# Forty-eight partitions of wq loaded in transfers of eight partitions: a decode kernel of attention and MLP on one core

## The chip, the cores and the metric

The kernel runs on one core of a Trainium2 chip. The metric is the device time of one execution in microseconds (us); lower is better. A profile is one more execution, recorded by the hardware profiler. Its times count from the span's start, which is the first instruction.

## What is computed

One decode step: attention with a cache (A) and a small MLP (B), mixed by a gate, for 8 batch rows of 448 values in bf16. A uses the last 1,024 positions of the caches; 16 query heads share 8 heads of K and V.

```python
# x: 8 x 1 x 448; k_cache, v_cache: 8 x 8 x 4096 x 256; wq: 448 x 4096; wo: 4096 x 448
def _A_ref(x, k_cache, v_cache, wq, wo):
    W = min(4096, max(256, Sk // 4))                      # 1024
    q = (x @ wq).reshape(B, Sq, Hq, Dh).transpose(0, 2, 1, 3)
    k = jnp.repeat(k_cache[:, :, Sk - W:, :], rep, axis=1)
    v = jnp.repeat(v_cache[:, :, Sk - W:, :], rep, axis=1)
    p = softmax(jnp.einsum("bhqd,bhkd->bhqk", q, k) * Dh ** -0.5)
    o = jnp.einsum("bhqk,bhkd->bhqd", p, v)
    return o.transpose(0, 2, 1, 3).reshape(B, Sq, Hq * Dh) @ wo
def _B_ref(x, w1, b1, w2, b2):
    return gelu(layernorm(x) @ w1 + b1) @ w2 + b2
g = sigmoid((x * gate_w).sum(-1, keepdims=True))
out = g * a + (1 - g) * b
```

## The kernel before

Nearly all large loads are issued from SyncE's queue, in program order: w1, its remainder w1_t and w2 (L159 to L164), then wq (L165 to L168), then K, V and wo in the order of the list `units` (L170 to L200). wq has 448 rows of 4,096 columns. Its first 384 rows lie in the tile `wq_sb`, of 128 partitions: partition p holds rows 3p, 3p + 1 and 3p + 2, which are one run of 24,576 bytes in memory. L167 loads it in three transfers (DC is 3), the c-th of which takes row 3p + c, 8,192 bytes, into every partition. The other 64 rows are `wq_t` (L168), half a row in each partition.

K and V come in 64 units of 1 MB, two batch rows of one head at a time, as 128 partitions of 8,192 bytes (`load`, L141). The last unit of V comes as two halves. A pool of 12 buffers takes them; `issue_to` (L182) issues a load when a buffer has been read. The eight parts of wo, 448 KB each, are issued between them (L187); wo's last part is the last load of all. The framework gives the loads eight semaphores in turn, so a load waits until the load that had the same semaphore before it has landed. The three small loads at the start (x, b1 and b2, L156 to L158), the load of gate_w (L288, eight copies of a row into eight partitions) and half of the output go through ScalarE's queue, and take semaphores from the same eight.

TensorE works in the order of the program: the MLP (L311, L347), then q (L370 to L384), where the rounds c = 0, 1 and 2 read `wq_sb[:, c, :]` on all partitions and the fourth reads `wq_t`, then the steps over K and V. One step of K transposes half a unit (L407), VectorE copies it (L412), and 16 small matmuls give scores (L433). After the four units of a head comes the softmax (L444 to L496), and with a lag of three steps the products with V (L508), the scaling (L519) and the projection with wo (L533), which adds into one bank. At the end VectorE mixes A and B (L577) and two transfers write the output (L581).

Of the kernel before, what the change touches and what calls it, by code (L numbers as in the profile page):

```python
# [16 lines left out]
def kernel(  # L17
# [15 lines left out]
    nc = tc.nc  # L33
    P = nc.NUM_PARTITIONS
# [73 lines left out]
    wq_sb = big.tile([P, DC, HD], BF16, name="wq_sb")  # L108
# [54 lines left out]
    w2_v = w2_sb[:].rearrange("p (h k) n -> p h k n", h=2)  # L163
    nc.sync.dma_start(w2_v, B_w2.rearrange("(h p k) n -> p h k n", h=2, k=NH))  # L164
    wq_v = A_wq[0:DM, :].rearrange("(p c) n -> p c n", c=DC)  # L165
    for c in range(DC):
        nc.sync.dma_start(wq_sb[:, c, :], wq_v[:, c, :])  # L167
    nc.sync.dma_start(wq_t[:], A_wq[DM:D, :].rearrange("r (h n) -> (r h) n", h=2))  # L168

    VU = (SPG + LAG) // TB  # L170
# [441 lines left out]
```

## Time and profile before

| | |
|---|---|
| time, median of 3 runs | 196.78 us (196.78 to 196.85) |
| the profiled execution's own time | 196.92 us |
| its span | 195.2 us |
| granted TensorE clock, mean | 0.768 |
| TensorE busy | 164.2 us (84%) |
| VectorE busy | 113.1 us (58%) |
| bytes moved by DMA | 78.14 MB, 400 GB/s on average |
| wq_sb loads: count, size, median us to landing | 3, 1,024 KB, 12.1 |
| K loads: count, size, median us to landing | 32, 1,024 KB, 18.3 |

In the rows of the profile, PE is TensorE, PEld its weight loads, DVE VectorE, ACT ScalarE, and SPq and ACTq are the queues of SyncE and ScalarE from which DMAs are issued. The page gives each engine's busy share, the DMA queues with their packets, megabytes and the share of 16 engines' span that the packets took, and the chain of work that ended last. A row of a table by stretches has the stretch and its length, each engine's busy time with the number of instructions, the granted clock, the mean busy share of the 16 DMA engines and GB/s. Behind a row of the timeline stands, in brackets, the idle time before it and what ended that.

### The profile page before, as it was taken

To read this page: it belongs to the slowest core of one execution; us is meant where nothing else is said; L and a number is where in the kernel's file an instruction comes from. 1 tells how busy PE (TensorE), PEld (TensorE's weight loads), DVE (VectorE), ACT (ScalarE), POOL (GpSimd) and SP (SyncE) were. 2 spreads that over 40 slices of the span, in tenths; PEclk is the share of its full clock that TensorE was granted. 3 is DMA by queue.
4 is the path that set the end of the run, shared out by engine and by line. 5 is a ranking of instruction groups with operands and counts; after the bars stand their busy time and mean duration, and the time that the engine had idled before them with its cause. 6 is when DMAs were issued, how large, how long until landed. Compare 5 with 4: busy or idle time off the path is not lost.

```text
span 195.2 us, 7355 instructions
## 1 busy us (share of the span) xinstructions
PE 164.2 (84%) x3417; PEld 153.6 (79%) x3417; DVE 113.1 (58%) x255; ACT 6.4 (3%) x13; POOL 2.8 (1%) x16
## 2 busy tenths in 40 slices
PE   2677799988899796958999898988898989989752
PEld 1565799988899796957999797978897989989541
DVE  3122189996477653764559674964586646766401
ACT  5000000000000000010000000000000000000000
POOL 5000000000000000000000000000000000000000
PEclk9999889997569855585569996995599655699555
DMA  6999999999999999999999999999999999999940
GB/s 215 412 426 425 425 413 426 426 423 420 421 426 422 417 425 426 425 417 431 423 423 419 422 425 428 418 421 418 425 430 417 421 425 430 426 420 425 394 176 5
DMA packets 12769, 78.14 MB, mean 400 GB/s; under 512 B 1330, under 2 KB 3523, under 8 KB 4164
## 3 DMA queue, kind: packets, MB, share of 16 engines
q1 hardware_dynamic: 12688, 77.67, 95.4%
q8 instruction: 26, 0.43, 0.8%
q10 hardware_dynamic: 52, 0.02, 0.0%
q14 instruction: 3, 0.02, 0.0%
HBM read 77.68 MB, written 0.01 MB: 398 GB/s over the span
## 4 chain that ended last, share of the span: by engine, by line
DMA 91%; PE 6%; SPq 1%; issue 0%; DVE 0%
DMA kv<-in_A_k_cache_dram 47%; DMA kv<-in_A_v_cache_dram 19%; DMA wo_sb<-in_A_wo_dram 18%; DMA wq_sb<-in_A_wq_dram 7%; PE ktp L407 4%; PE grp L433 1%; PE A_bank L533 0%; PE grp L508 0%; SPq L167 0%; PE grp L422 0%; SPq L164 0%; DVE res L577 0%; SPq L159 0%; SPq L162 0%; SPq L148 0%
## 5 line engine op out<-in xcount | busy, mean ns | idle before, releaser
L412 DVE COPY kt<-ktp 128x1024 bf16<-128x1024 bf16 x128 | 84.4, 687 | 44.4 <-PE ktp L407 43.9
L407 PE MATMUL ktp<-ident,kv 128*128 128x128 bf16 x1024 | 89.0, 257 | 7.9 <-DMA kv<-in_A_k_cache_dram 6.7
L407 PEld LDWEIGHTS <-kv 128*128 128x128 bf16 x1024 | 78.0, 118 | 10.9 <-DMA kv<-in_A_k_cache_dram 7.9
L508 PE MATMUL grp<-e,kv 128*128 128x4 bf16 x1024 | 35.6, 166 | 2.6 <-DMA kv<-in_A_v_cache_dram 2.5
L508 PEld LDWEIGHTS <-kv 128*128 128x128 bf16 x1024 | 32.6, 101 | 5.6 <-DMA kv<-in_A_v_cache_dram 2.8
L433 PE MATMUL grp<-qT,kt 128*128 128x4 bf16 x1024 | 36.6, 166 | 0.3 <-DVE kt L412 0.2
L433 PEld LDWEIGHTS <-kt 128*128 128x128 bf16 x1024 | 34.6, 100 | 1.8 <-issue 0.6
L482 ACT ACTIVATE e<-grp 128x256 bf16<-128x256 f32 x8 | 3.1, 383 | 161.8 <-PE grp L475 161.8
L491 PE MATMUL A_bank<-zs,onesf 128*128 128x16 f32 x16 | 3.6, 299 | 4.5 <-DVE zs L487 4.5
L491 PEld LDWEIGHTS A_bank<-zs,onesf 128*128 128x128 f32 x16 | 2.8, 218 | 5.1 <-DVE zs L487 5.1
L533 PE MATMUL A_bank<-wo_sb,ot 128*8 128x224 bf16 x64 | 5.5, 305 | 0.8 <-DMA wo_sb<-in_A_wo_dram 0.5
L321 PE MATMUL h_ps<-yT,w_sb 128*128 128x8 bf16 x42 | 4.2, 195 | 1.2 <-DMA w_sb<-in_B_w_dram 1.2
L495 DVE RECIPROCAL rz<-A_bank 128x16 f32<-128x16 f32 x8 | 2.1, 258 | 5.4 <-PE A_bank L491 5.4
L519 DVE TENSOR_TENSOR ot<-grp,rz 128x32 bf16<-128x32 f32 x8 | 1.5, 186 | 6.4 <-PE grp L508 6.4
L487 DVE TENSOR_REDUCE zs<-e 128x16 f32<-128x256 bf16 x8 | 4.8, 602 | 0.0
L353 PE MATMUL b_ps<-w_sb,hT 128*8 128x224 bf16 x28 | 2.8, 388 | 2.4 <-DVE b_ps L349 2.4
L338 DVE COPY z<-h_ps 128x112 f32<-128x112 f32 x1 | 0.3, 275 | 7.7 <-PE h_ps L329 7.7
L321 PEld LDWEIGHTS <-w_sb 128*128 128x128 bf16 x42 | 3.6, 152 | 1.3 <-DMA w_sb<-in_B_w_dram 1.3
L475 PE MATMUL grp<-diag,onesb 128*128 128x256 bf16 x8 | 2.5, 308 | 2.2 <-DVE diag L469 1.9
L353 PEld LDWEIGHTS <-hT 128*8 128x8 bf16 x28 | 1.8, 121 | 3.0 <-DVE hT L344 2.2
L446 DVE TENSOR_REDUCE pm<-grp 128x16 f32<-128x256 f32 x8 | 3.3, 415 | 0.6 <-PE grp L433 0.6
L533 PEld LDWEIGHTS <-ot 128*8 128x8 bf16 x64 | 2.6, 93 | 1.3 <-issue 0.4
(82 smaller groups left out, 53.6 us busy)
## 6 DMA issues: line engine op xcount, KB each, us to landing
kv<-in_A_k_cache_dram SPq DMA_DIRECT2D x32, 1024.0 KB, 18.3
kv<-in_A_v_cache_dram SPq DMA_DIRECT2D x31, 1024.0 KB, 18.3
wo_sb<-in_A_wo_dram SPq DMA_DIRECT2D x8, 448.0 KB, 18.3
wq_sb<-in_A_wq_dram SPq DMA_DIRECT2D x3, 1024.0 KB, 12.1
w_sb<-in_B_w_dram SPq DMA_DIRECT2D x1, 1568.0 KB
w_sb<-in_B_w_dram SPq DMA_DIRECT2D x1, 1344.0 KB, 5.9
kv<-in_A_v_cache_dram SPq DMA_DIRECT2D x2, 512.0 KB, 19.8
wq_t<-in_A_wq_dram SPq DMA_DIRECT2D x1, 512.0 KB, 14.5
```

The costliest lines, as they stand in the source:

```text
L321: nc.tensor.matmul(o, lhsT=cols(w1_sb[:, c, h * FH : (h + 1) * FH]), rhs=yT[:, c, :], start=(c == 0), stop=False,)
L353: nc.tensor.matmul(b_ps[CP * j : CP * j + NB, 0:DN], lhsT=M["hT"][:, k * NB : (k + 1) * NB] if k < NF else onesb[0:1, 0:NB], rhs=w2_sb[:, ...
L407: nc.tensor.transpose(ktp[:, c * P : (c + 1) * P], K[:, h * HC + c, j * P : (j + 1) * P], ident[:],)
L412: nc.vector.tensor_copy(kt[:, j, :], ktp[:])
L433: nc.tensor.matmul(G[g][:, s : s + RU], lhsT=kt[:, j, c * P : (c + 1) * P], rhs=qT[:, j, g, bu * TB : (bu + 1) * TB, :].rearrange("p t i - ...
L446: nc.vector.reduce_max(pm[:], G[g][:, S0 : S0 + NC * R].rearrange("p (c r) -> p r c", r=R), axis=AXIS.X,)
L475: nc.tensor.matmul(G[g][:, S0 : S0 + NC * R].rearrange("p (c r) -> p c r", c=NC), lhsT=onesb[:], rhs=diag[g % 2][:].unsqueeze(1).to_broadc ...
L482: nc.scalar.activation(e[:], G[g][:, S0 : S0 + NC * R], ACT.Exp)
L487: nc.vector.reduce_sum(zs[:], E[g][:].rearrange("p (c r) -> p r c", r=R), axis=AXIS.X)
L491: nc.tensor.matmul(zc, lhsT=onesf[:], rhs=zs[:], start=False, stop=True, skip_group_check=True)
L508: nc.tensor.matmul(G[g][:, o : o + RU], lhsT=V[:, cc, :].rearrange("p (q j) -> p j q", j=NJ)[:, j, :], rhs=E[g][:, cc * R + bu * RU : cc * ...
L533: nc.tensor.matmul(A_bank[CP * j : CP * j + NB, 0:DN], lhsT=ot[:].rearrange("p j (b i) -> p j i b", i=rep)[:, h, i, :], rhs=wo_sb[g][:, k, ...
```

## The change

wq's 128 partitions are divided into partitions 0 to 79 and 80 to 127. The first 80 are still loaded in three transfers, one for each c, now of 80 partitions x 8,192 bytes. The last 48 are loaded in six transfers of eight partitions, each partition its whole run of 24,576 bytes, all three c at once. Two of these stand ahead of each transfer of 80. So nine transfers take the place of three; the bytes are the same. No other line differs, and the lines behind move by ten.

```diff
     wq_v = A_wq[0:DM, :].rearrange("(p c) n -> p c n", c=DC)
+
+
+    SH = 48
+    PM = P - SH
+    small = [(p, p + 8) for p in range(PM, P, 8)]
     for c in range(DC):
-        nc.sync.dma_start(wq_sb[:, c, :], wq_v[:, c, :])
+        for lo, hi in small[2 * c : 2 * c + 2]:
+            nc.sync.dma_start(
+                wq_sb[lo:hi].rearrange("p c n -> p (c n)"),
+                wq_v[lo:hi].rearrange("p c n -> p (c n)"),
+            )
+        nc.sync.dma_start(wq_sb[0:PM, c, :], wq_v[0:PM, c, :])
     nc.sync.dma_start(wq_t[:], A_wq[DM:D, :].rearrange("r (h n) -> (r h) n", h=2))
```

## The prediction

> **What bounds the kernel now.** I read the chain of work that ended last first, then the queues' part of the page, then stretches near the end, then the trace's records of single DMA packets. The chain and the queues, from the page:
>
> ```profile
> DMA 91%; PE 6%; SPq 1%; issue 0%; DVE 0%
> ...
> q1 hardware_dynamic: 12688, 77.67, 95.4%
> q8 instruction: 26, 0.43, 0.8%
> ```
>
> The span ends with a DMA in 91% of its chain, and queue q1, SyncE's, keeps the 16 DMA engines busy for 95.4% of the span. TensorE is busy for 84%, but the chain names it for 6%. So the time is set by the DMA engine that finishes last. Stretches of the tail (first column the stretch in us, last two the mean busy share of the 16 engines and GB/s):
>
> ```profile
> 150.00:180.00 30.00, 27.46 (x585) 26.19 (x582) 18.87 (x38) 0.38 (x1) 0.00 (x0) 0.71 1.02 425
> 180.00:184.60 4.60, 3.04 (x63) 2.36 (x63) 2.26 (x11) 0.38 (x1) 0.00 (x0) 0.50 1.00 412
> 185.50:189.20 3.70, 2.09 (x72) 1.92 (x70) 0.26 (x1) 0.00 (x0) 0.00 (x0) 0.50 0.52 203
> 189.70:190.90 1.20, 0.58 (x16) 0.50 (x16) 0.04 (x1) 0.00 (x0) 0.00 (x0) 0.50 0.09 33
> ```
>
> The engines do not end together: all 16 are busy to 184.6, about eight (0.52 of 16) from 185.5 to 189.2, one or two (0.09) after 189.7. What follows the last of them, from the timeline of the tail:
>
> ```profile
> 191.37 0.91 PE L533 MATMUL A_bank<-wo_sb,ot 128*8 128x224 bf16 x8 [0.54 <-DMA wo_sb<-in_A_wo_dram]
> ...
> 192.32 0.44 DVE L577 SCALAR_TENSOR_TENSOR res<-A_bank,gg,bvec 64x224 bf16<-64x224 f32 x1 [1.26 <-PE A_bank L533]
> 192.79 0.38 SPq L581 DMA_DIRECT2D out_dram<-res  x1
> ```
>
> The last packet of wo ends at 190.98 and lands at 191.33; 3.9 us of fixed tail follow, to 195.2. The profiled execution took 196.92 us, 1.7 more than its span. The median of the runs, 196.78, is 0.07% below it, so I forecast against 196.92 without a correction.
>
> **Which engine ends last, and why.** A packet record has a start, a duration, a queue and a size, but no engine. In the steady part an 8,192 B packet takes 309 ns and the next starts 3 ns before it ends, so packets can be linked into 16 chains by their times. The finish of a transfer on one engine is a 4 B packet. From one 4 B packet to the next, eight 8,192 B packets, is 2.453 us on an undisturbed chain. Two things mark chains:
>
> - The load of gate_w, eight rows on ScalarE's queue, leaves one 896 B packet (41 ns) on each of eight chains between 63.27 and 63.57; there the interval is 2.497. I call these the gate eight.
> - Each of the 26 instruction packets of q8 (16,384 B, about 930 ns) holds up one chain: an interval of 3.87 instead of 2.453, 1.41 us lost. They go round eight chains in turn; two of these take four, the others three.
>
> The ends of the sixteen chains:
>
> ```
> gate eight, no instruction packets   184.68 184.76 184.80 185.14 185.15 186.49
> gate eight, three, and four          189.44 190.23
> the rest, none                       185.13 185.40
> the rest, three (five chains)        189.34 189.39 189.43 189.43 189.60
> the rest, four                       190.98
> ```
>
> These give 8 to 9 busy chains at 187 and 1.4 on average from 189.7 to 190.9, as the stretches do (0.52 and 0.09 of 16). The lateness is the instruction packets: about 4.2 us for three. Two of the eight late chains are among the gate eight. The chain of 190.23 is alone in its phase by over 100 ns, so I am sure of it; that of 189.44 has a neighbour 5 ns away.
>
> **The change, part by part.** *Bytes.* Before, each chain carries 8 rows of 8,192 B of each of three wq transfers: 24 packets. After, the three transfers of 80 rows give each chain 5 rows each, 15 packets; six transfers of eight rows of 24,576 B go to eight chains only, one row each. I take these eight to be the gate eight, since that load too has eight rows. They get 6 x 24,576 B, the bytes of 18 packets, so 33 against 24: nine more, 9 x 306 ns = +2.75 us. The other eight lose nine: -2.75 us. Longer runs may save a little: a 4,096 B packet every 157 ns and an 8,192 B one every 306 make the fixed part some 7 ns, at most 12 x 7 = 0.08 us for six rows.
>
> [...]
>
> *Issues.* SyncE issues nine wq transfers for three: six more at 0.49 us (the median of L167). Eight semaphores are used in turn, so a transfer waits for the one eight before. K's first load now waits for the first 80-row transfer, which the gate eight pass at about 10.6 + 2 x 0.92 + 5 x 0.306 = 14.0 (10.6 is the end of w2). With 0.35 to landing and 1.05 from issue to packets (L159: 0.80 to 1.85), K's packets are there at 15.4. The other eight run dry at 10.6 + 15 x 0.306 + 8 x 0.157 = 16.4. One us of cover; without it those engines would lose time of which they have 2.75 us spare. Cost 0. Later, the other eight run up to 10 us ahead of the last chain; issue to landing is 18.3 us (median of the K loads), so their queues stay filled.
>
> *TensorE.* The q matmuls read all partitions, so the first of three rounds, which began at 18.7, waits for the sixth small transfer at about 19.5. K's transposes stand behind them in TensorE's order; K's first load, on which they waited for 1.33 us until 23.54, lands about 2.7 us later too. TensorE and the copies after it move later with the data. Cost 0 at the end, since the tail waits on wo; if TensorE had no slack to catch up the price would again be at most these 2.7 us, not a sum of both.
>
> *Sum.* Gate eight: 187.4 to 189.2, and the two with instruction packets 192.2 and 190.23 + 2.75 = 192.98. The rest: 182.4 to 186.9 and 188.2. The last end moves from 190.98 to 192.9, +1.9 us. **196.92 + 1.9 = 198.8 us**, 1% slower. The change evens the halves on average, but adds work to the two late chains that stand in the wrong half. Bounds of this case: if the packet count goes round differently, the last is a chain of three, 192.2, giving 198.0; 199.1 with a little more delay at the start.
>
> **The rivals.**
>
> *A. Eight adjacent partitions are a narrow door; slower by far.* Eight engines now write at once into eight neighbouring partitions, which before held for no large transfer. No row shows it at size. The nearest are the 896 B packets: six of x's, into eight neighbouring partitions, began within 18 ns; five took 39 or 40 ns, like lone ones, and the first 61. That speaks for no limit, but so few bytes may only have been buffered. If four rows have to share what one chain moves alone, a row takes 4 x 0.918 = 3.67 us, 2.75 more; six transfers add 16.5 us to the gate eight: 192.9 + 16.5 = 209.4, a time of 215.3 us. Any partial sharing falls between 198.8 and that. [...]
>
> *B. The late chains are all in the other half; faster.* If the eight small-transfer chains hold none of the instruction packets (because SyncE's eight rows go elsewhere than ScalarE's, or these packets use other engines in another execution), the loaded chains end at 186.49 + 2.75 = 189.2 and the late ones at 188.2: 1.8 us earlier, 195.1 us. The tipping point is one late chain of four packets among the eight: it alone makes it slower. For it speaks that six of the eight late chains do stand in the other half; against it the chain of 190.23, marked by both signs.
>
> *C. The small transfers are spread over 16 engines after all.* Then no chain's bytes change and the time stays within 0.2 us of 196.9. Against it: the gate load used eight chains.
>
> **How the numbers follow.** The forecast gets 0.46 (198.0 to 199.1), A in full or part 0.32 (199.5 to 216), B 0.14, C 0.08 and the like. A change of 0.2% is about what a measurement of this kernel can tell from none; the cases give faster 0.14, same 0.07, slower 0.79. To hold 8 in 10 the range takes the forecast, most of A and part of C, leaving out B: 196.7 to 216.
>
> **What would show it.** Right: in the tail, a stretch with two chains (0.12) left after 190, the last wo landing near 193.2, wq's later loads landing some 2.7 us later, and chains of the gate eight with 33 packets' worth of wq. A: packets of the small transfers that take well over 0.92 us per 24,576 B, first K landing 15 us later. B: the last wo landing before 190 and a staircase with a higher second step. Wrong would be the forecast, too, if q8's packets fell on other chains, or if TensorE rather than a DMA released the last o_proj.

## The result, and the profile after

The changed kernel takes 218.07 us (median; 218.04 to 219.41) against 196.81 us of the kernel before, measured beside it: a ratio of 1.110, 95% interval 1.105 to 1.114. It is 21.3 us slower. The forecast was 198.8 us, with a range up to 216.0; the time lies 2.1 us outside, and 2.8 us beyond the price of rival A.

The profiled execution took 218.07 us, its span 216.4. The shares of the chain that ended last, from the page of the kernel after, stand against DMA 91% before:

```profile
DMA 76%; PE 15%; DVE 4%; issue 2%; SPq 1%; ACT 0%
```

The chain in order of time (start, length, what) has two pieces of a new size, both of wq, and its last load is wo, as before:

```profile
3.00 11.78 DMA wq_sb<-in_A_wq_dram
14.80 26.49 DMA wq_sb<-in_A_wq_dram
...
196.47 15.86 DMA wo_sb<-in_A_wo_dram
```

The timeline shows that wo still releases the last projection:

```profile
212.37 0.91 PE L543 MATMUL A_bank<-wo_sb,ot 128*8 128x224 bf16 x8 [0.53 <-DMA wo_sb<-in_A_wo_dram]
```

So a DMA still sets the end: the last wo packet ends at 211.99 instead of 190.98, 21.0 us later, and wq holds the chain until 41.3. In the 40 slices of the span (4.9 us each before, 5.4 us after), the engines' busy tenths and GB/s, before first:

```profile
DMA  6999999999999999999999999999999999999940
GB/s 215 412 426 425 425 413 426 426 423 420 421 426 422 417 425 426 425 417 431 423 423 419 422 425 428 418 421 418 425 430 417 421 425 430 426 420 425 394 176 5
```

and after:

```profile
DMA  6989998999999999999999999999999999999930
GB/s 227 425 108 179 89 197 91 333 423 423 421 420 420 426 421 427 420 424 423 426 421 420 427 420 427 421 423 418 429 423 423 421 423 423 430 420 426 377 149 10
```

The busy row is nearly as full as before; in the row of GB/s five slices, the third to the seventh, fall to 89 to 197. The stretch in which its packets move, and a later one, first in the kernel after (last two columns: busy share of the 16 DMA engines, GB/s):

```profile
10.20:37.50 27.30, 5.95 (x63) 4.59 (x62) 2.17 (x8) 0.30 (x1) 0.00 (x0) 0.71 1.03 141
18.90:25.90 7.00, 0.00 (x0) 0.00 (x0) 0.08 (x1) 0.00 (x0) 0.00 (x0) 0.70 1.03 109
37.50:42.00 4.50, 2.52 (x89) 2.46 (x90) 0.00 (x0) 0.00 (x0) 0.00 (x0) 0.50 0.95 291
60.00:100.00 40.00, 36.24 (x783) 34.35 (x781) 27.46 (x58) 0.77 (x2) 0.00 (x0) 0.79 1.01 422
```

and in the kernel before:

```profile
10.20:37.50 27.30, 23.50 (x482) 21.60 (x481) 14.64 (x30) 0.30 (x1) 0.00 (x0) 0.94 1.01 423
60.00:100.00 40.00, 34.21 (x648) 32.39 (x645) 23.42 (x49) 0.93 (x3) 0.00 (x0) 0.63 1.01 423
```

The share is 1.03 and 1.01, so the engines did not lack work; but what they move fell from 423 GB/s to 141, and from 60 us on it is as before. Nearly all the loss lies in the stretch of wq. From 10.2 to 37.5 the missing bytes are 27.3 us x (423 - 141) GB/s = 7.7 MB, which take 18 us at 423 GB/s; from 37.5 to 42.0 another 1.4 us are lost in the same way. By the packet records the bytes are 19.8 us behind the kernel before from there to the end. The last packet is 21.0 us behind, because the chains of packets are not late by the same amount; the part on the prediction comes back to that. TensorE waits for wq, as its line for q shows, before and after:

```profile
L377 PE MATMUL q_ps<-xT,wq_sb 128*128 128x8 bf16 x96 | 2.6, 167 | 0.0
L387 PE MATMUL q_ps<-xT,wq_sb 128*128 128x8 bf16 x96 | 2.9, 168 | 20.9 <-DMA wq_sb<-in_A_wq_dram 20.9
```

The packet records tell how. The 48 rows of 24,576 B, which three 8,192 B packets' time would make 0.92 us, take 2.01 to 4.10 us, 3.23 on average. Nor are the other packets spared: of the 8,192 B packets between 10 and 45 us, 309 ns each before but for five held up by instruction packets and a few up to 316, 367 of 574 now take over 340 ns. Some 39 lie within 5% of four times 306 ns and 32 within 5% of five times; the others lie below and between, and none takes over 1,572. Packets that take up to five times the normal time, while all engines are busy, look like something shared by up to five.

### The profile page after: what moved, and what is told of

Its sections match the earlier page's. It is cut to its first block, busy times and chain, and to the rows that moved or that the text cites. A ratio compares the mean times of both kernels' runs of the same rounds, so it can differ in the third digit from the quotient of the medians.

```text
span 216.4 us, 7364 instructions
## 1 busy us (share of the span) xinstructions
PE 163.7 (76%) x3417; PEld 152.7 (71%) x3417; DVE 113.1 (52%) x255; ACT 6.4 (3%) x13; POOL 2.8 (1%) x16
## 4 chain that ended last, share of the span: by engine, by line
DMA 76%; PE 15%; DVE 4%; issue 2%; SPq 1%; ACT 0%
DMA kv<-in_A_k_cache_dram 33%; DMA wq_sb<-in_A_wq_dram 18%; DMA wo_sb<-in_A_wo_dram 16%; PE ktp L417 9%; DMA kv<-in_A_v_cache_dram 8%; PE grp L443 2%; DVE kt L422 2%; PE q_ps L387 1%; PE grp L518 1%; PE A_bank L543 1%; SPq L164 1%; DVE gsum L302 0%; PE A_bank L501 0%; DVE diag L479 0%; DVE prod L301 0%
## 5 line engine op out<-in xcount | busy, mean ns | idle before, releaser
L417 PE MATMUL ktp<-ident,kv 128*128 128x128 bf16 x1024 | 87.7, 254 | 7.7 <-DMA kv<-in_A_k_cache_dram 7.4
L417 PEld LDWEIGHTS <-kv 128*128 128x128 bf16 x1024 | 76.8, 117 | 11.1 <-DMA kv<-in_A_k_cache_dram 8.8
L518 PEld LDWEIGHTS <-kv 128*128 128x128 bf16 x1024 | 32.7, 101 | 5.1 <-issue 3.0
L387 PE MATMUL q_ps<-xT,wq_sb 128*128 128x8 bf16 x96 | 2.9, 168 | 20.9 <-DMA wq_sb<-in_A_wq_dram 20.9
L387 PEld LDWEIGHTS <-wq_sb 128*128 128x128 bf16 x96 | 2.7, 104 | 21.2 <-issue 20.8
L399 DVE TENSOR_SCALAR qT<-q_ps 128x128 bf16<-128x128 f32 x2 | 0.5, 298 | 27.3 <-PE q_ps L387 27.3
L543 PE MATMUL A_bank<-wo_sb,ot 128*8 128x224 bf16 x64 | 6.2, 335 | 0.8 <-DMA wo_sb<-in_A_wo_dram 0.5
```

The costliest lines, as they stand in the source:

```text
L387: nc.tensor.matmul(q_ps[:, k * NB : (k + 1) * NB], lhsT=w, rhs=xs, start=(c == 0 and k == 0), stop=(c == DC), skip_group_check=True,)
L417: nc.tensor.transpose(ktp[:, c * P : (c + 1) * P], K[:, h * HC + c, j * P : (j + 1) * P], ident[:],)
L518: nc.tensor.matmul(G[g][:, o : o + RU], lhsT=V[:, cc, :].rearrange("p (q j) -> p j q", j=NJ)[:, j, :], rhs=E[g][:, cc * R + bu * RU : cc * ...
L543: nc.tensor.matmul(A_bank[CP * j : CP * j + NB, 0:DN], lhsT=ot[:].rearrange("p j (b i) -> p j i b", i=rep)[:, h, i, :], rhs=wo_sb[g][:, k, ...
```

## The experiments

The theory, **doors**, was my assumption when the runs were planned; neither kernel's trace shows it by itself. It supposes that groups of four partitions are written through a common door, which passes no more than what one chain moves alone (8,192 B per 306 ns), that a transfer of all 128 partitions is dealt out so that each chain has its own door, and that eight neighbours have two doors, so that four chains wait at each. Rivals: a **long run** of 24,576 B is slow in itself; **reading** neighbouring rows is slow; the **imbalance** of the chains, or the eight semaphores, starves something. The times of the kernel before on the same chips were 196.72 to 196.94 us (medians).

Kernels that change a line of the changed kernel, in the table as "after":

| kernel | us | ratio (95%) | rows of 24,576 B: mean, range, us | longest 8,192 B packet before 60 us, ns |
|---|---|---|---|---|
| after | 218.07 | 1.110 (1.105 to 1.114) | 3.23, 2.01 to 4.10 | 1,572 |
| e1, rows in three packets | 220.74 | measured once | - | 1,611 |
| e2, six apart | 208.32 | 1.060 (1.057 to 1.063) | 1.73, 1.18 to 2.79 | 1,064 |
| e3, 80 and 48 | 204.96 | 1.040 (1.038 to 1.043) | - | 1,078 |
| e4, 16 neighbours | 207.59 | measured once | 2.66, 1.51 to 3.30 | 1,202 |
| e5, written six apart | 208.93 | 1.061 (1.052 to 1.070) | 1.71, 1.08 to 2.66 | 940 |
| e6, written to neighbours | 219.56 | 1.115 (1.112 to 1.118) | 3.22, 2.03 to 3.93 | 1,662 |
| e7, 32 in neighbours | 213.72 | 1.085 (1.072 to 1.099) | 3.17, 2.15 to 3.99 | 1,508 |
| e8, 32, four apart | 204.88 | 1.040 (1.030 to 1.051) | 1.62, 1.11 to 1.86 | 856 |

In every kernel some 8,192 B packets of 760 to 860 ns stand beside an instruction packet, as before.

**e1, the long run taken away.**

```diff
-    wq_sb = big.tile([P, DC, HD], BF16, name="wq_sb")
+    wq_sb = big.tile([P, DC, HD + 32], BF16, name="wq_sb")
...
-                wq_sb[lo:hi].rearrange("p c n -> p (c n)"),
-                wq_v[lo:hi].rearrange("p c n -> p (c n)"),
+                wq_sb[lo:hi, :, 0:HD], wq_v[lo:hi],
...
-        nc.sync.dma_start(wq_sb[0:PM, c, :], wq_v[0:PM, c, :])
+        nc.sync.dma_start(wq_sb[0:PM, c, 0:HD], wq_v[0:PM, c, :])
```

> The six small transfers keep their partitions and bytes, but each row goes as three packets of 8,192 B (wq_sb's rows are padded by 64 B). Doors theory (groups of partitions are written through a common door that moves only what one DMA chain moves, 8,192 B per 306 ns, so four of eight neighbours share one): no change, 216 to 220 us, and these packets take about 4 to 5 x 309 ns = 1.2 to 1.5 us. Rival, long runs (a packet of 24,576 B is slow in itself): packets of 309 ns, about 199 us.

220.74 us, 0.7 above what I expected, packets up to 1.6 us, and 141 GB/s from 10.2 to 37.5, as in the changed kernel. Without any long run nothing is won, so the run's length is not the cause.

**e2, other partitions for the same rows.**

```diff
-    small = [(p, p + 8) for p in range(PM, P, 8)]
+    small = [slice(PM + j, P, 6) for j in range(6)]
...
```

(The loop below takes a slice in place of two bounds.)

> Each small transfer takes eight partitions six apart (80, 86, ... 122) instead of eight neighbours; rows, sizes, counts and order as in the changed kernel. Doors theory: the eight rows reach seven or eight doors, so a row takes 0.92 to 1.84 us instead of 3.2, and the time is 199 to 204 us (198.8 by the bytes per chain, the rest by sharing doors with the other eight chains' own packets). Long runs: 218 us, rows still about 3.2 us. Imbalance alone (half the engines, eight semaphores): 218 us too.

208.32 us: 9.8 us of the 21.3 are gone with nothing changed but which partitions go together, and rows take 1.73 us. Imbalance alone can't do that. Its stretch of wq:

```profile
10.00:27.50 17.50, 6.27 (x66) 4.77 (x65) 2.17 (x8) 0.30 (x1) 0.00 (x0) 1.00 1.03 237
```

The time is 4 us above what I expected of the doors; e3 tells why.

**e3, no eight-row transfer at all.**

```diff
-        for lo, hi in small[2 * c : 2 * c + 2]:
...
+        nc.sync.dma_start(wq_sb[PM:P, c, :], wq_v[PM:P, c, :])
         nc.sync.dma_start(wq_sb[0:PM, c, :], wq_v[0:PM, c, :])
```

> The 48 partitions come in three transfers of 48 x 8,192 B, one behind... ahead of each transfer of 80, on all 16 chains; every chain carries the bytes it carried before. Doors theory: partitions 0 to 79 load half of the doors twice as heavily as the others, 80 to 127 the other half, so each part takes up to as long as a whole transfer of 128: at most 3 x 2.45 = 7.3 us more, 199 to 204 us, with packets of 600 ns and over. Long runs and imbalance: no long run and no imbalance is left, 196.9 to 197.4 us with packets of 309 ns.

204.96 us, 8.2 more than before, though every chain carries its old bytes in its old packets; that is 1.0 us above the range that I expected. Blocks of 80 and of 48 neighbouring partitions are slow without any small transfer: where the packet records can be linked into chains, the five packets of a transfer of 80 take 3.0 us on average, for 1.53, and the three of 48 take 2.0, for 0.92. The stretch of wq:

```profile
10.20:25.00 14.80, 8.05 (x129) 6.50 (x128) 2.16 (x8) 0.30 (x1) 0.00 (x0) 0.92 1.03 212
```

Half of 423 GB/s, at full busy share.

**e4, all chains loaded alike.**

```diff
-    small = [(p, p + 8) for p in range(PM, P, 8)]
+    small = [(p, p + 16) for p in range(PM, P, 16)]
...
-        for lo, hi in small[2 * c : 2 * c + 2]:
+        for lo, hi in small[c : c + 1]:
```

> The 48 partitions come in three transfers of 16 neighbours, each a run of 24,576 B, so all 16 chains carry one row of each and no chain is loaded more. Doors theory: 16 neighbours have four doors, four rows to a door, a row takes about 3.2 us as before, three of them in every chain: 3 x 2.3 = 7 us and what the transfers of 80 lose, 204 to 212 us. Imbalance alone: 197 us. Long runs: rows of 3.2 us too, 204 us.

207.59 us with rows of 2.66 us, where I had expected 3.2: without imbalance it is still slow, and inside the range that the doors gave.

**e5 and e6, the two sides of a transfer apart.** Of e2's two sides, e5 keeps the written one and e6 the read one; the other is as in the changed kernel. Both therefore compute q from rows of wq in a wrong order.

```diff
-    small = [(p, p + 8) for p in range(PM, P, 8)]
+    small = [(PM + 8 * j, slice(PM + j, P, 6)) for j in range(6)]
...
-                wq_sb[lo:hi].rearrange("p c n -> p (c n)"),
-                wq_v[lo:hi].rearrange("p c n -> p (c n)"),
+                wq_sb[sl].rearrange("p c n -> p (c n)"),           # e6: wq_sb[lo : lo + 8]
+                wq_v[lo : lo + 8].rearrange("p c n -> p (c n)"),   # e6: wq_v[sl]
```

> Each small transfer reads eight neighbouring rows of wq, as the changed kernel does, but writes them to partitions six apart (q is computed from wq rows in the wrong order). Doors at the written partitions: as with both sides six apart, 207 to 210 us, rows of 1.7 us. Rival, reading: if the neighbouring rows in memory were what is slow, 218 us and rows of 3.2 us.

> The reverse: rows six apart are read, and written to eight neighbouring partitions (q is computed from wq rows in the wrong order). Doors at the written partitions: 217 to 220 us, rows of 3.2 us. Rival, reading: 207 to 210 us, rows of 1.7 us.

208.93 and 219.56 us. The stretches of wq, e5 first, then e6:

```profile
10.00:27.40 17.40, 6.17 (x65) 4.67 (x63) 2.17 (x8) 0.30 (x1) 0.00 (x0) 1.00 1.02 240
```

```profile
10.20:37.50 27.30, 6.20 (x65) 4.69 (x64) 2.17 (x8) 0.30 (x1) 0.00 (x0) 1.00 1.02 138
```

The speed follows the partitions that are written, not the rows that are read: 240 GB/s as with both sides six apart (237 in e2), 138 as in the changed kernel (141).

**e7 and e8, how the groups are made.** Both take SH = 32 and four small transfers. e7 keeps neighbours; in e8 no two partitions of a transfer stand in the same group of four neighbours.

```diff
-    SH = 48
+    SH = 32
...
-    small = [(p, p + 8) for p in range(PM, P, 8)]
+    small = [slice(PM + j, P, 4) for j in range(4)]       # e8 alone
...
-        for lo, hi in small[2 * c : 2 * c + 2]:
+        for lo, hi in small[4 * c // 3 : 4 * (c + 1) // 3]:
```

> Only 32 partitions (96 to 127) in four transfers of eight neighbours, the other 96 in three transfers. Doors theory: four rows instead of six in each of the eight chains, and 96 rows of three 32-partition groups load the doors less unevenly than 80: about 2/3 of the 21.3 us or less, 207 to 212 us, rows of about 3 us.

> The same 32 partitions in four transfers of eight partitions four apart (96, 100, ... 124). [...] Groups of four: rows of 0.92 us alone and 1.84 us beside the other chains' own packets, 199 to 204 us. [...]

213.72 us, 1.7 above what I expected, and 204.88 us, 0.9 above; 150 GB/s from 10 to 33 us, and 244 from 10 to 23.8. That eight partitions four apart have a door each was an assumption of e8's forecast; its rows took 1.62 us on average. None takes over 1.86 us, two rows' time, so at most two seem to meet. If doors were contiguous blocks of eight partitions, two rows of one transfer would share a door, up to 1.84 us for each, and the other chains' packets would come on top; groups of four fit better, and e12 measures such rows without that company.

The last four start from the kernel before, not from the changed one. **e9, the long run in one whole transfer:**

```diff
-    for c in range(DC):
-        nc.sync.dma_start(wq_sb[:, c, :], wq_v[:, c, :])
+    nc.sync.dma_start(
+        wq_sb[:].rearrange("p c n -> p (c n)"), wq_v.rearrange("p c n -> p (c n)")
+    )
```

> The kernel before, with wq's 384 rows in a single transfer of 128 partitions x 24,576 B: the long run without any part transfer. Doors theory: in a transfer of all 128 partitions no two chains meet at a door, so a row takes 3 x 306 = 0.92 us and the time stays within 0.3% of the kernel before, or gains up to 0.1 us from fewer packets. If long runs were slow: 16 or more us more.

196.84 us, ratio 1.0009 (0.9999 to 1.0019): no measurable difference. The 128 rows of 24,576 B took 912 ns in the median, 1,007 at most, so a chain passes 24,576 B / 0.912 us = 26.9 GB/s in such a transfer, and the 16 together 426 from 10.2 to 18.5.

**e10 and e11, one split by halves and one by even and odd.**

```diff
     for c in range(DC):
-        nc.sync.dma_start(wq_sb[:, c, :], wq_v[:, c, :])
+        for sl in (slice(0, 64), slice(64, P)):           # e11: slice(0, P, 2), slice(1, P, 2)
+            nc.sync.dma_start(wq_sb[sl, c, :], wq_v[sl, c, :])
```

> The kernel before, with each of wq's three transfers split into partitions 0 to 63 and 64 to 127, four rows of 8,192 B per chain, all chains loaded alike. Doors theory with half of the doors in each half of the partitions: each part of 64 takes as long as a whole transfer, 3 x 2.45 = 7.3 us more, 203 to 205 us, 8,192 B packets of 612 ns. No doors: six issues instead of three, hidden, 197 us.

> The same, but split into the even and the odd partitions, so that each part has rows for all doors alike. If the rows of a part are dealt to the chains so that each meets its own door: 197 us, packets of 309 ns. If they are dealt in blocks in the order of the partitions (0, 2, 4, 6 to the first chain): chains in step meet two at a door although all doors are used, packets of 612 ns, up to 204 us. This tells what is still open about the transfers of 80.

204.55 us (1.040; 1.038 to 1.042) against 197.83 (1.006; 1.004 to 1.008). The stretches, halves first:

```profile
10.20:25.00 14.80, 7.95 (x126) 6.40 (x126) 2.17 (x8) 0.30 (x1) 0.00 (x0) 1.00 1.02 224
```

```profile
10.20:18.50 8.30, 5.89 (x64) 4.65 (x62) 1.78 (x7) 0.30 (x1) 0.00 (x0) 1.00 1.01 424
```

The same count and size of transfers: by halves they move 224 GB/s, with packets of close to twice 306 ns (median 594); by even and odd 424, with every packet of wq at 309 ns. A transfer of half the partitions is not slow because it is half, but because of which half. In e11 the span is 195.1 us and the last wo packet ends at 190.91, as before; the 1.1 us that its runs take more lie outside the span (197.94 us for that execution), and why is open.

**e12, rows moved to eight chains with the doors kept even.**

```diff
+    small = [slice(32 * j + 3, 32 * j + 32, 4) for j in range(4)]
     for c in range(DC):
-        nc.sync.dma_start(wq_sb[:, c, :], wq_v[:, c, :])
+        for sl in small[4 * c // 3 : 4 * (c + 1) // 3]:
+            nc.sync.dma_start(
+                wq_sb[sl].rearrange("p c n -> p (c n)"),
+                wq_v[sl].rearrange("p c n -> p (c n)"),
+            )
+        for sl in (slice(0, P, 2), slice(1, P, 4)):
+            nc.sync.dma_start(wq_sb[sl, c, :], wq_v[sl, c, :])
```

> Moves rows to eight chains as the changed kernel does, but with the doors kept even: the partitions 3, 7, ... 127 come in four transfers of eight, four apart, each partition a run of 24,576 B; the even partitions and 1, 5, ... 125 in three transfers each of 8,192 B runs. The eight chains carry 6 packets' worth more (18 - 6 + 12 - ... = 30 for 24), the others 6 less. Forecast's sum of bytes per chain: the late chain among the eight goes from 190.23 to 192.07, the last one of the others to 189.1, so 1.1 us more, 197.9 us, or 199 with the 1.1 us that six more issues cost in the even and odd split. Doors theory: the first two of the four meet no other chain at their doors (rows of 0.92 us), the last two share them (1.84 us), so up to 1.8 us on top, 199 to 201 us; nothing as in the changed kernel, no row over 2 us.

199.66 us (1.018; 1.012 to 1.023). The rows of the small transfers, from the packet records:

```
partitions 3, 7, ... 31       all eight rows 912 ns
partitions 35, 39, ... 63     all eight rows 912 ns
partitions 67, 71, ... 95     1,139 to 1,701 ns
partitions 99, 103, ... 127   1,834 to 1,891 ns
```

The first 16 rows take what a row takes in e9, as if they met nobody. The last eight take twice the time (2 x 912 = 1,824), as if each shared with one other for all its length, and those between lie between. So eight partitions four apart within 32 did not hold each other up, which fits eight doors. More can be worked out from these times and e10, where 64 neighbours moved at about the rate of eight chains (224 GB/s against 8 x 26.9 = 215), but it is my reading and no run shows it alone: partitions 32 to 63 would use the same doors as 0 to 31, which the eight chains of the small transfers would have to themselves, and 64 to 127 the doors of the other eight chains. The last wo packet ends at 192.93, 1.95 us later than before.

## Why the prediction was wrong, point by point

- **What bounds the kernel** held: the last wo packet sets the end in both kernels, the tail after it is 4.2 us before and 4.4 after, and the 21.0 us that it comes later are nearly all of the 21.3.
- **"They get 6 x 24,576 B, the bytes of 18 packets"**, at 306 ns each, is the step that failed. The count was right, the price was not: the six rows of a chain take on average 2.36, 3.10, 3.10, 4.01, 3.06 and 3.77 us, 19.4 together, where I had 5.5. This is 13.9 us.
- **"15 packets" of the transfers of 80**, also at 306 ns, was wrong too, and no rival of mine had it. In the eight chains the stretches between the small transfers take 3.3 and 3.4 us for five rows, where I had 1.53, and what follows the last small row, five rows and wq_t, takes 5.2 us (36.4 to 41.6) where I had 2.8: together 6.0 us. The sum is then 2.75 + 13.9 + 6.0 = 22.7 us for these chains; the late ones among them, at 189.44 and 190.23 before, would end at 212.1 and 212.9, and the last two chains ended at 211.78 and 212.00.
- **Rival A**, given 0.32, comes nearest to what the runs show: rows are slow by the partitions that they are written to (e5 and e6: 1.71 and 3.22 us). Its price of 16.5 us for the small rows was 13.9, probably because the chains do not arrive in step (the eight rows of a transfer start 0.3 to 2.0 us apart) and rows overlap only in part; and it left out 6.0 us of the transfers of 80. So its 215.3 fell 2.8 us short and the range missed. The four rows that share, on which its price and the upper end of the range rest, were an assumption that no run shows; in their place the runs showed rows of 3.23 us on average for eight neighbours, 3.5 times the 912 ns of e9. I let 896 B packets, at 39 to 61 ns, speak against it; they showed only that so small a write was not held up visibly.
- **"The change evens the halves on average"** took it that the other eight chains gain 2.75 us. They didn't: of the 8,192 B packets that ran while all eight rows of a small transfer were under way, 105 took over 340 ns, up to 1,559 for 309. By the doors theory, a row that another chain carries still goes through its own door. With the bytes 19.8 us behind on average and the gate eight 22.7, the others are some 16.9 us late.
- **Which chains end last** held, as far as the times of the chains tell, which are all that matches those of the two kernels here; that the small transfers use the gate eight was an assumption. By the packet records the sixteen chains of the changed kernel end at 201.7 and 202.2, five at 206.1 to 206.4, seven at 207.4 to 209.1, and two at 211.8 and 212.0. The ends before, with 22.7 us added for the gate eight and 16.9 for the others, are two at 202.0 and 202.3, five at 206.2 to 206.5, seven at 207.4 to 209.2, and two at 212.1 and 212.9. The sign that I had named, two chains (0.12) left at the end, stands there 21 us later:

```profile
210.70:211.90 1.20, 0.59 (x16) 0.51 (x16) 0.02 (x1) 0.00 (x0) 0.00 (x0) 0.50 0.12 45
```

- **The forecast's sum without the doors' price.** e12 comes nearest to the forecast's own case: its 6 packets more (1.84 us) and 1.5 us of sharing (rows of 1.42 and 1.87 us for 0.912 on average) on the chain of 190.23 make 193.5, and the last packet ended at 192.93. Which chain that was I did not follow, so this agrees with the sum of bytes and does not prove it.
- **Cost 0 for the issues** stands: the busy share is 1.03 over the stretch, so the engines had packets to work on. **TensorE** waits 20.9 us for wq and has made it up by the tail, as assumed.
- Open: how the rows of 80 neighbouring partitions are dealt to the chains. That blocks of 80 and 48 together run at half speed is shown (e3), the order within them isn't.

## What to carry to other kernels

Before a transfer over all partitions is cut, look at which partitions each part writes: parts that are interleaved (even and odd) kept 424 GB/s here, while cuts into neighbouring blocks of 8 to 80 partitions fell to between a quarter (109) and about a half (224) of that. A busy share near 1 does not show that the DMA engines are at their rate (here 1.03 at 141 GB/s and 1.01 at 423); read GB/s, and the durations of packets of one size, beside it. And a rival that would put 16 us in place of 2 deserves a look at how little the row that seems to contradict it can tell, here packets a ninth of the smallest in question.

## What the runs showed of the hardware that was not expected

- Two disjoint halves of the partitions moved at 224 GB/s when they were cut at 64 (e10), and at 424, without loss of rate, when they were interleaved (e11).
- Where two rows of 24,576 B met, each took about twice 912 ns (1,834 to 1,891 in e12), and in the changed kernel no 8,192 B packet took much over five times 306 ns (1,572 at most). That fits a door shared in even parts by up to five.
- One run of 24,576 B in place of three of 8,192 B gains nothing that can be measured (e9, ratio 1.0009).
